# Two layers of cached attention and a gated feed-forward: the tail of one V load in each layer goes to loads of 8, 8 and 112 rows

## The chip, the cores and the metric

The kernel runs on one core of one Trainium2 chip, in one launch. The metric is the device time in microseconds; lower is better. Before the change it is 707.6 us, the median of three runs (707.39 to 707.8).

## The reference

A decoding step with one token for each of four sequences. Two layers, which share their weights and their cache, each compute attention over a cache of 4096 keys and a gated feed-forward, both on a normalised input and added to it:

```python
def _A_ref(x, k_cache, v_cache, wq, wo):        # x (4, 1, 512), caches (4, 8, 4096, 128)
    q = (x @ wq).reshape(B, Sq, 32, 128).transpose(0, 2, 1, 3)
    k = jnp.repeat(k_cache, 4, axis=1)
    v = jnp.repeat(v_cache, 4, axis=1)
    p = softmax(jnp.einsum("bhqd,bhkd->bhqk", q, k) * 128 ** -0.5)
    o = jnp.einsum("bhqk,bhkd->bhqd", p, v)
    return o.transpose(0, 2, 1, 3).reshape(B, Sq, 4096) @ wo

def _B_ref(x, w1, w3, w2):                      # 512 -> 1792 -> 512
    return (silu(x @ w1) * (x @ w3)) @ w2

for layer in range(2):
    x = x + _A_ref(layernorm(x), k_cache, v_cache, wq, wo)
    x = x + _B_ref(layernorm(x), w1, w3, w2)
```

Everything is float32.

## The kernel before, in words

One SBUF tile `arena` of 216 KB in each of 128 rows holds all that is loaded; `KB` is 256 floats, so one unit is 1 KB of a row. Loads stand in a list `plan`, written in the order in which they are to be issued, and `pump` (lines 136 to 150) issues from its front on the queue of SyncE as long as `take` finds room in the arena. `done` gives the room of a load back when its last piece has been used, and calls `pump` again. So the order of the transfers is the order of the list, and a transfer starts when TensorE has used up an earlier one. Each DMA bears on one of eight completion semaphores in turn.

The cache of one of the eight heads of K, or of V, is 8 MB: 64 KB in each of the 128 rows, as a rule one load (128 x 16384 floats). Layer 0 takes the heads 0 to 7, layer 1 takes them 7 to 0; the V of head 7 stays in the arena from one layer to the next, and so the V loads of layer 0 are of the heads 0 to 7, those of layer 1 of the heads 6 to 0. K of a head stands ahead of V of the head before it. Between the layers come the smaller loads of wo, w1, w3 and w2, at the end again w1, w3 and w2.

`scores` (line 342) multiplies the queries with K into `s_ps`; `factors` and `exponents` make the softmax of it, `turn_p` transposes the weights, and `weigh` (line 388) multiplies them with V into `o_ps`. `weigh` does it in two halves `f`, each of four pieces of V: the eight pieces, 8 KB of a row each, are the keys ("v", layer, head, 0 to 7). After the first half ScalarE empties `o_ps` (line 401), after the second VectorE does (line 403). TensorE goes through scores of one head, then V of the head before it, and waits for each load's completion semaphore before the first product that reads it.

In the names of the profile `arena<-in_v`, `arena<-in_kt`, `arena<-in_w` are these loads; line 143 issues them all, line 351 is a product with K and line 394 one with V.

Of the kernel before, what the change touches and what calls it, by code (L numbers as in the profile page):

```python
# [16 lines left out]
P = 128  # L17
# [12 lines left out]
KB = 256  # L30
ARENA = 216
TURN = HKV - 1
SPLIT = 3
SCRATCH = 64


@with_exitstack
def tile_decode_layers(ctx: ExitStack, tc: tile.TileContext, x, kt, v, wq, wo, w1, w3, w2, out):
    nc = tc.nc
# [5 lines left out]
    arena = const.tile([P, ARENA * KB], F32, name="arena")  # L45
# [9 lines left out]
    def take(n, at=None):  # L55
        if at is not None and at < WO:
            return at
        for i, (lo, size) in enumerate(free):
            if at is None and state["next"] > ring["to"]:

                end = min(lo + size, PT)
                if lo < WO + 4 and end > WO:
                    if WO - lo >= n:
                        end = WO
                    else:
                        lo = WO + 4
                if end - lo < n:
                    continue
                a = lo
                lo, size = free[i]  # L70
            else:
                a = lo if at is None else at
            if lo <= a and a + n <= lo + size:
                free[i:i + 1] = [(p, s) for p, s in ((lo, a - lo), (a + n, lo + size - a - n)) if s]
                return a
        return None
# [59 lines left out]
    def pump():  # L136
        while state["next"] < len(plan):
            src, per, keys, at = plan[state["next"]]
            n = src.shape[-1] // KB
            a = take(n, at)  # L140
            if a is None:
                return
            nc.sync.dma_start(arena[:, a * KB:(a + n) * KB], src)  # L143
            i = state["next"]
            if i == 0:
                nc.sync.dma_start(xt[:8], x[:8])
            left[i] = (len(keys), a, n)
            for j, key in enumerate(keys):
                where[key] = (a + j * per, per, i)
            state["next"] += 1  # L150
# [5 lines left out]
    def done(*key):  # L156
        i = where[key][2]
        k, a, n = left[i]
        left[i] = (k - 1, a, n)
        if k == 1:  # L160
            give(a, n)
            pump()

    def vacate(*key):
        a, n, _ = where[key]
        give(a, n)
        pump()

    xt = const.tile([P, KC, B], F32, name="xt")
    nc.scalar.dma_start(xt[8:], x[8:])  # L170
    pump()

    ident = const.tile([P, P], F32, name="ident")
# [425 lines left out]
```

## Time and profile before

| | |
|---|---|
| median of three runs | 707.6 us |
| the profiled execution | 708.3 us, of it a span of 706.5 us |
| TensorE's matmuls busy | 414.7 us (59%) |
| VectorE busy | 80.4 us (11%) |
| ScalarE busy | 38.3 us (5%) |
| moved by DMA | 299.37 MB, 424 GB/s in the mean |
| TensorE's granted clock, mean | 0.787 |

The span runs from the first to the last instruction; the profiled execution's own time is that and 1.8 us around it, and it is 0.7 us above the median. A row of a DMA queue gives its packets, its MB and the time of its packets as a share of 16 DMA engines over the span. A group's row gives busy time, the mean of one instruction in ns, and the idle time ahead of it with what ended most of that.

### The profile page before, as it was taken

To read this page: it belongs to the slowest core of one execution; us is meant where nothing else is said; L and a number is where in the kernel's file an instruction comes from. 1 tells how busy PE (TensorE), PEld (TensorE's weight loads), DVE (VectorE), ACT (ScalarE), POOL (GpSimd) and SP (SyncE) were. 2 spreads that over 40 slices of the span, in tenths; PEclk is the share of its full clock that TensorE was granted. 3 is DMA by queue.
4 is the path that set the end of the run, shared out by engine and by line. 5 is a ranking of instruction groups with operands and counts; after the bars stand their busy time and mean duration, and the time that the engine had idled before them with its cause. 6 is when DMAs were issued, how large, how long until landed. Compare 5 with 4: busy or idle time off the path is not lost. (4 is left out here: it accounts for less than half of the span.)

```text
span 706.5 us, 7210 instructions
## 1 busy us (share of the span) xinstructions
PE 414.7 (59%) x3250; PEld 147.4 (21%) x3250; DVE 80.4 (11%) x274; ACT 38.3 (5%) x87; POOL 2.9 (0%) x10
## 2 busy tenths in 40 slices
PE   3545354546555463547788886365564646367687
PEld 1111021112111120212243222021120212122235
DVE  2001010101001010101111021002010101010111
ACT  0000000000000000002010000000000000000101
POOL 0000000000000000000000000000000000000000
PEclk9977776777677687768899978679787878788679
DMA  9999999999999999999999999999999999999996
GB/s 384 459 405 468 416 423 450 423 428 438 439 423 428 453 416 438 446 401 435 407 404 371 407 437 448 430 428 435 434 424 449 424 423 454 427 416 428 423 425 283
DMA packets 13716, 299.37 MB, mean 424 GB/s; under 512 B 1655, under 2 KB 1783, under 8 KB 6007
## 3 DMA queue, kind: packets, MB, share of 16 engines
q1 hardware_dynamic: 13552, 298.92, 99.0%
q8 instruction: 25, 0.41, 0.2%
q10 hardware_dynamic: 135, 0.01, 0.0%
q14 instruction: 4, 0.03, 0.0%
HBM read 298.85 MB, written 0.07 MB: 423 GB/s over the span
## 5 line engine op out<-in xcount | busy, mean ns | idle before, releaser
L394 PE MATMUL o_ps<-arena 128*32 128x512 f32 x1024 | 149.4, 734 | 146.7 <-DMA arena<-in_v 132.2
L351 PE MATMUL s_ps<-arena,qpad 128*32 128x512 f32 x1024 | 151.5, 747 | 80.8 <-DMA arena<-in_kt 80.8
L394 PEld LDWEIGHTS o_ps<-arena 128*32 128x32 f32 x1024 | 37.8, 132 | 256.9 <-issue 226.1
L351 PEld LDWEIGHTS s_ps<-arena,qpad 128*32 128x32 f32 x1024 | 39.7, 133 | 174.7 <-issue 161.6
L403 DVE SCALAR_TENSOR_TENSOR p<-o_ps,parts,p 128x512 f32<-128x512 f32 x16 | 12.0, 751 | 270.6 <-PE o_ps L394 250.8
L358 DVE TENSOR_REDUCE top<-s_ps 128x1 f32<-128x512 f32 x16 | 11.1, 691 | 192.1 <-PE s_ps L351 192.1
L406 PE MATMUL m_ps<-sel,p 128*128 128x16 f32 x128 | 17.0, 265 | 14.3 <-DVE p L403 14.2
L415 PE MATMUL x_ps<-arena,oT 128*4 128x256 f32 x256 | 18.8, 431 | 6.3 <-DMA arena<-in_wo 4.3
L295 PE MATMUL o_ps<-arena,xpad 128*32 128x512 f32 x112 | 14.8, 649 | 12.0 <-DMA arena<-in_wq 12.0
L401 ACT ACTIVATE p<-o_ps,parts 128x512 f32<-128x512 f32 x16 | 11.0, 687 | 196.6 <-PE o_ps L394 187.9
L406 PEld LDWEIGHTS m_ps<-sel,p 128*128 128x128 f32 x128 | 15.5, 191 | 28.9 <-DVE p L403 28.9
L382 PE MATMUL t_ps<-ident,p 128*128 128x128 f32 x64 | 11.4, 305 | 13.5 <-ACT p L376 13.5
L369 ACT ACTIVATE f<-d 128x1 f32<-128x1 f32 x16 | 3.2, 203 | 252.8 <-DVE d L367 252.8
L376 ACT ACTIVATE p<-s_ps,top 128x512 f32<-128x512 f32 x16 | 10.9, 684 | 82.5 <-PE m_ps L406 82.5
L239 PE MATMUL m_ps<-ident,rows 128*32 128x128 f32 x70 | 13.1, 293 | 0.0
L383 DVE COPY arena<-t_ps 128x512 f32<-128x512 f32 x16 | 11.1, 691 | 8.8 <-PE t_ps L382 8.8
L382 PEld LDWEIGHTS t_ps<-ident,p 128*128 128x128 f32 x64 | 7.3, 150 | 19.5 <-ACT p L376 15.6
L446 PE MATMUL s_ps<-arena,xpad 128*32 128x192 f32 (+1 forms) x128 | 9.7, 421 | 1.4 <-DMA arena<-in_w 1.1
L446 PE MATMUL o_ps<-arena,xpad 128*32 128x192 f32 (+1 forms) x128 | 9.4, 404 | 1.3 <-DMA arena<-in_w 1.2
L239 PEld LDWEIGHTS m_ps<-ident,rows 128*32 128x32 f32 x70 | 8.3, 121 | 5.4 <-issue 3.0
L415 PEld LDWEIGHTS x_ps<-arena,oT 128*4 128x4 f32 x256 | 6.1, 93 | 15.3 <-DMA arena<-in_wo 5.0
L295 PEld LDWEIGHTS o_ps<-arena,xpad 128*32 128x32 f32 x112 | 3.5, 119 | 20.8 <-DMA arena<-in_wq 12.9
(94 smaller groups left out, 134.1 us busy)
## 6 DMA issues: line engine op xcount, KB each, us to landing
arena<-in_kt SPq DMA_DIRECT2D x4, 4096.0 KB, 18.5
arena<-in_v SPq DMA_DIRECT2D x4, 4096.0 KB, 39.0
arena<-in_kt SPq DMA_DIRECT2D x9, 1024.0 KB, 12.1
arena<-in_w SPq DMA_DIRECT2D x15, 512.0 KB, 8.6
arena<-in_wq SPq DMA_DIRECT2D x1, 7168.0 KB, 40.2
arena<-in_v SPq DMA_DIRECT2D x3, 2048.0 KB, 37.6
arena<-in_wo SPq DMA_DIRECT2D x1, 4096.0 KB, 24.2
arena<-in_kt SPq DMA_DIRECT2D x2, 2048.0 KB, 20.8
```

Source lines behind the costliest of these rows:

```text
L239: nc.tensor.matmul(m_ps[turn["m"] ^ 1][0:32, 384:512], rows, ident, start=True, stop=True)
L295: nc.tensor.matmul(ps[32 * k:32 * k + 32, :], xpad[:, k, lo:lo + 32], w[:, k, :], start=first, stop=last)
L351: nc.tensor.matmul(s_ps[32 * b:32 * b + 32, :], qpad[:, b, lo:lo + 32], k[:, j, :], start=(blk == 0), stop=(blk == NB - 1))
L358: nc.vector.tensor_reduce(top[:, 0:1], s_ps, axis=AX.X, op=ALU.max, negate=True)
L382: nc.tensor.transpose(t_ps[:, i, :], p[:, i * P:(i + 1) * P], ident)
L383: nc.vector.tensor_copy(pT.rearrange("p i r -> p (i r)"), t_ps.rearrange("p i r -> p (i r)"))
L394: nc.tensor.matmul(o_ps[32 * b:32 * b + 32, :], pT[:, i, 32 * b:32 * b + 32], w[:, b, :], start=(i == 0), stop=(i == NI - 1))
L401: nc.scalar.activation(p, o_ps, AF.Copy, scale=st["parts"][:, 0:1])
L403: nc.vector.scalar_tensor_tensor(p, o_ps, st["parts"][:, 1:2], p, op0=ALU.mult, op1=ALU.add)
L406: nc.tensor.matmul(flat(m), p[:, j * P:(j + 1) * P], sel[:, j].rearrange("p h b -> p (h b)"), start=(j == 0), stop=(j == 3))
L415: nc.tensor.matmul(x_ps[r:r + B, e * 256:e * 256 + 256], left(2 * i + n), w(n)[:, e * 256:e * 256 + 256], start=first, stop=last)
L446: nc.tensor.matmul(ps[32 * j:32 * j + 32, lo:lo + n], x32[:, k, :], w[:, j * n:(j + 1) * n], start=(k == 0), stop=(k == KC - 1))
```

## The change

A load whose first key stands in `SHARES` is split: its rows are loaded up to `m` KB as before, by one DMA of 128 rows, and the last 24 or 32 KB of each row by three more, of rows 0 to 7, 8 to 15 and 16 to 127. That is V of head 5 in layer 0 (64 = 40 + 24 KB of a row) and V of head 3 in layer 1 (32 + 32 KB). Bytes, places in the arena and everything computed are the same.

```diff
+SHARES = {("v", 0, 5, 0): 24, ("v", 1, 3, 0): 32}
...
-            nc.sync.dma_start(arena[:, a * KB:(a + n) * KB], src)
             i = state["next"]
+            m = n - SHARES.get(keys[0], 0)
+            nc.sync.dma_start(arena[:, a * KB:(a + m) * KB], src[:, 0:m * KB])
+
+            for lo, hi in ((0, 8), (8, 16), (16, P)) if m < n else ():
+                nc.sync.dma_start(arena[lo:hi, (a + m) * KB:(a + n) * KB], src[lo:hi, m * KB:])
             if i == 0:
                 nc.sync.dma_start(xt[:8], x[:8])
```

Lines below move down by five (394 becomes 399). On the queue of SyncE, around V of head 5 in layer 0 (the row 128x16384 of `in_v` that waits for DMAHW7; DMAHW0 to 7 are the completion semaphores, PE that of TensorE), there stood:

```order
L143 DMA arena<-in_v 128x16384 [waits DMAHW5_49,PE_49]
L143 DMA arena<-in_kt 128x16384 [waits DMAHW6_49,PE_49]
L143 DMA arena<-in_v 128x16384 [waits DMAHW7_49,PE_49]
L143 DMA arena<-in_kt 128x16384 [waits DMAHW0_49,PE_49]
L143 DMA arena<-in_v 128x16384 [waits DMAHW1_49,PE_49]
L143 DMA arena<-in_v 128x8192 [waits DMAHW2_49,PE_49]
```

Now there stands:

```order
L146 DMA arena<-in_v 128x16384 [waits DMAHW5_49,PE_49]
L146 DMA arena<-in_kt 128x16384 [waits DMAHW6_49,PE_49]
L146 DMA arena<-in_v 128x10240 [waits DMAHW7_49,PE_49]
L149 DMA arena<-in_v 8x6144 [waits PE_49]
L149 DMA arena<-in_v 8x6144
L149 DMA arena<-in_v 112x6144
L146 DMA arena<-in_kt 128x16384 [waits DMAHW0_49,PE_49]
L146 DMA arena<-in_v 128x16384 [waits DMAHW3_49,DMAHW2_49,DMAHW4_49,DMAHW1_49,PE_49]
```

One DMA has become four, and the V load two rows further on, which takes the room of this one, waits for four landings in place of one.

On TensorE, the products with V of head 5 in layer 0 (the rows with `o_ps`, ahead of them the scores of head 6) stood so:

```order
L351 MATMUL s_ps<-arena,qpad 32x512 [waits DMAHW0_49,DVE_49]
L351 MATMUL s_ps<-arena,qpad 32x512 x31
L394 MATMUL o_ps<-arena 32x512 [waits DMAHW1_49,DVE_49]
L394 MATMUL o_ps<-arena 32x512 x15
L394 MATMUL o_ps<-arena 32x512 [waits Activation_49]
L394 MATMUL o_ps<-arena 32x512 x15
L406 MATMUL m_ps_120<-sel,p 128x16 [waits DVE_49]
```

Now they stand so:

```order
L356 MATMUL s_ps<-arena,qpad 32x512 [waits DMAHW0_49,DVE_49]
L356 MATMUL s_ps<-arena,qpad 32x512 x31
L399 MATMUL o_ps<-arena 32x512 [waits DMAHW1_49,DVE_49]
L399 MATMUL o_ps<-arena 32x512 x15
L399 MATMUL o_ps<-arena 32x512 [waits Activation_49]
L399 MATMUL o_ps<-arena 32x512 x3
L399 MATMUL o_ps<-arena 32x512 [waits DMAHW4_49,DMAHW3_49,DMAHW2_49]
L399 MATMUL o_ps<-arena 32x512 x11
L411 MATMUL m_ps_120<-sel,p 128x16 [waits DVE_49]
```

The first 20 of the 32 products wait for the 128-row load alone, the last 12 for the three new loads as well. In layer 1 the same wait stands at the start of the second half, after 16 products.

## The prediction

> **What bounds the kernel now.** I read the page's head and DMA rows first, then the groups that wait, the chain, and last the stretches of the windows view.
>
> ```profile
> span 706.5 us, 7210 instructions
> DMA  9999999999999999999999999999999999999996
> q1 hardware_dynamic: 13552, 298.92, 99.0%
> q8 instruction: 25, 0.41, 0.2%
> q10 hardware_dynamic: 135, 0.01, 0.0%
> ...
> L394 PE MATMUL o_ps<-arena 128*32 128x512 f32 x1024 | 149.4, 734 | 146.7 <-DMA arena<-in_v 132.2
> L351 PE MATMUL s_ps<-arena,qpad 128*32 128x512 f32 x1024 | 151.5, 747 | 80.8 <-DMA arena<-in_kt 80.8
> ```
>
> The queue row says it: q1, which carries every load, takes 99.0% of 16 engines' span, and TensorE's two big groups stand idle 132.2 us for V and 80.8 us for K. No engine of the core is the bound. The last landing sets the end, as the chain's last pieces say:
>
> ```profile
> 628.95 43.48 DMA arena<-in_v
> ...
> 672.49 29.53 DMA arena<-in_w
> 702.02 0.14 issue
> 702.15 1.65 PE x_ps L502 x48
> ```
>
> A load is complete when the slowest of its DMA engines is, so what counts is not their mean but the last of the 16. The windows view shows how far apart they are (its last two columns are the busy share of the 16 engines and GB/s):
>
> ```profile
> core 0: us, PE busy (x) PEld busy (x) DVE busy (x) ACT busy (x) POOL busy (x), PEclk, DMA share, GB/s
> 180.00:240.00 60.00, 31.92 (x218) 9.58 (x214) 5.63 (x18) 1.87 (x5) 0.00 (x0) 0.70 1.01 435
> 372.00:378.00 6.00, 3.72 (x44) 1.68 (x48) 0.42 (x1) 0.00 (x0) 0.00 (x0) 0.89 1.02 400
> 378.00:384.00 6.00, 5.39 (x57) 2.41 (x49) 0.59 (x3) 0.00 (x0) 0.00 (x0) 0.83 1.00 365
> 384.00:390.00 6.00, 5.91 (x50) 3.37 (x54) 1.48 (x11) 0.85 (x3) 0.55 (x1) 1.00 0.96 337
> ...
> 698.00:699.00 1.00, 1.00 (x29) 0.80 (x33) 0.18 (x1) 0.00 (x0) 0.00 (x0) 1.00 0.97 389
> 699.00:699.50 0.50, 0.50 (x22) 0.50 (x12) 0.00 (x0) 0.00 (x0) 0.00 (x0) 1.00 0.83 336
> 700.00:700.50 0.50, 0.50 (x28) 0.45 (x24) 0.00 (x0) 0.00 (x0) 0.00 (x0) 1.00 0.54 217
> 701.00:701.50 0.50, 0.50 (x6) 0.34 (x4) 0.00 (x0) 0.00 (x0) 0.00 (x0) 1.00 0.54 188
> 701.50:702.00 0.50, 0.12 (x2) 0.00 (x0) 0.00 (x0) 0.00 (x0) 0.00 (x0) 1.00 0.35 135
> 702.50:703.00 0.50, 0.50 (x28) 0.50 (x20) 0.00 (x0) 0.00 (x0) 0.00 (x0) 1.00 0.07 25
> 703.00:703.50 0.50, 0.50 (x24) 0.25 (x16) 0.00 (x0) 0.00 (x0) 0.00 (x0) 1.00 0.00 0
> ```
>
> In steady state the 16 engines move 435 GB/s, 27.2 each. At the end all work until about 698.5 (0.97). By 700 to 700.5 the share is 0.54, nine of 16, and it is still 0.54 a microsecond later; the last one stops shortly before 703. So about seven engines are done some 3 us before the slowest. All carry the same bytes; what differs is small work such as the 25 instruction fetches (0.41 MB, 16 KB and so 0.6 us each at 27.2 GB/s). No view names the engines.
>
> **The change part by part.** First, which engines get what. The counts of the DMA rows tell it, with these:
>
> ```profile
> L143 SPq DMA_DIRECT2D arena<-in_kt x33: 327/328/607, 1.6 to 606.7; - x33
> L143 SPq DMA_DIRECT2D arena<-in_w x32: 327/328/837, 330.2 to 682.3; - x32
> L143 SPq DMA_DIRECT2D arena<-in_v x21: 327/328/425, 30.8 to 639.7; - x21
> L143 SPq DMA_DIRECT2D arena<-in_wo x5: 327/328/1021, 320.6 to 325.5; - x5
> L143 SPq DMA_DIRECT2D arena<-in_wq x2: 377/443/509, 0.7 to 2.4; - x2
> ```
>
> These are 93 loads of 128 rows, and with the store of the output 94 transfers. At one packet a row and one closing packet for each of 16 engines they make 94 x 144 = 13536 packets. q1 has 13552; the 16 left over are the one 8-row load of x: eight rows and eight closing packets, so eight engines with a row each. q10 agrees: 135 = 120 rows + 15. By the same division (the largest number up to 16 that divides the rows) the 112 rows go to 16 engines, seven each. Both new 8-row loads go, I take it, to the same eight engines. So of the tail, where each of 16 engines moved eight rows, eight engines ("the loaded eight") now move 1 + 1 + 7 = 9, and the others 7. At 27.2 GB/s a tail row of 24 KB (24,576 bytes) takes 0.90 us and one of 32 KB 1.20 us. The shift alone is thus 0.90 us more for the loaded eight and as much less for the others in layer 0, and 1.20 us each way in layer 1.
>
> Six more issues of 0.33 us lie on SP. They cost nothing, since SP then waits for TensorE, and the data engines are fed well ahead:
>
> ```profile
> 248.85 0.33 SPq L143 DMA_DIRECT2D arena<-in_v  x1
> 265.99 0.33 SPq L143 DMA_DIRECT2D arena<-in_kt  x1
> 276.56 5.85 PE L394 MATMUL o_ps<-arena 128*32 128x512 f32 x32 [10.63 <-DMA arena<-in_v]
> 286.98 0.33 SPq L143 DMA_DIRECT2D arena<-in_v  x1
> ...
> 579.28 6.38 PE L394 MATMUL o_ps<-arena 128*32 128x512 f32 x32 [10.10 <-DMA arena<-in_v]
> 586.52 3.64 PE L394 MATMUL o_ps<-arena 128*32 128x512 f32 x32 [0.86 <-ACT p L401]
> 590.23 0.33 SPq L143 DMA_DIRECT2D arena<-in_v  x1
> 599.04 1.94 PE L351 MATMUL s_ps<-arena,qpad 128*32 128x512 f32 x8 [4.84 <-DMA arena<-in_kt]
> ```
>
> SP issues nothing between 248.85 and 265.99; without that 17 us of cover the three would cost 1 us. The V load issued at 248.85 is in use at 276.56, 28 us later, when about one more load is queued.
>
> The wait that the change adds on TensorE, for the three tail loads, is behind work that can now start earlier: the first 40 or 32 of 64 KB land before the tail, so 10.63 us of idling becomes work begun earlier. That gains nothing by itself: the next product waits for its own load (4.84 us at 599.04). Were the tail late by more than that slack, the V product would delay the scores, but those wait for loads that are late by the same amount, since each DMA engine works its queue in order. Lateness of a DMA engine is therefore not hidden; it goes on to the end of the layer.
>
> Now the unknown cost. In a 128-row load 435 GB/s go to 128 rows: 27.2 GB/s to each engine, and as well 27.2 to each eight rows of SBUF. The rows do not tell to which of the two the limit belongs. If to the engine, an 8-row load takes 0.90 us (24 KB) or 1.20 (32 KB). If to eight neighbouring rows as a group, it takes eight times that: 7.2 or 9.6 us. These are the two ends. Nothing in this trace writes eight neighbouring rows from eight engines at length (the x load has 64 bytes a row), so no row is nearer to either; I take the mean, 4.05 and 5.4 us. The loaded eight are then later by 2 x 4.05 - 0.9 = 7.2 us in layer 0 and 2 x 5.4 - 1.2 = 9.6 us in layer 1. A gain from a faster 8-row load is excluded: no engine goes above 27.2 GB/s.
>
> The Trainium skill bears on this (SBUF — State Buffer, section "Door 1: The DMA port swizzle"): DMA bandwidth depends on how many of 16 ports the partitions reach; four neighbours, and the four 32 further on, share one, and partitions 0 to 3 alone got 27.6 GB/s. By it eight rows reach two ports and an 8-row load takes 3.6 or 4.8 us; by the same steps as below the time would be 717.8 us. No row here shows it.
>
> What comes off: at the end, seven engines have 3 us in hand, but eight are loaded, so at least one starts from the slower group, which ends 701.3 to 703: I take 2 us off in each layer at most, say 1.5 off layer 0 and 1.5 off layer 1. In the middle, between the layers, 400 GB/s falls to 365 and 337: (35 + 63) / 400 x 6 us = 1.5 us per engine, in which engines wait for issues and part of a delay can vanish. So 7.2 + 9.6 - 1.5 - 1.5 - 1.5 = +12.3 us. The profiled execution took 708.3 us, its span 706.5; the median of the runs is 707.6, and I add to that: 719.9, say **720 us**.
>
> **Rivals.** *No slowing of the 8-row loads, and no side wins.* The limit is the engine's. Then the loaded eight gain 0.90 and 1.20 us of work. Eight loaded against seven early means that one late engine at least gets more; if it is among the last, layer 1 ends 1.2 us later, if not up to 1.2 earlier. In layer 0 the like with 0.9. With opposite signs the time is 707.6 +- 1.4. For it: the last stretch holds one engine (0.07), of either kind. The same result comes if the change doesn't do what it says, because the 8-row loads use other engines each time: bytes then even out, 707.6.
>
> *Faster.* The limit is the engine's, and the loaded eight are the seven early ones and one of middling lateness. The others end 0.9 and 1.2 us sooner, and the early ones stay ahead (700.25 + 1.2 = 701.45, below 703 - 1.2 = 701.8). Time: 707.6 - 2.1 = 705.5. It decides as long as an 8-row load takes less than about twice 1.2 us: then the loaded eight are at 700.25 + 3.6 = 703.85, past today's end. For it: two groups, seven and nine, close to half and half. Against: nothing shows that the loaded eight are the early ones.
>
> *Slower by the shift alone.* The slowest engine is a loaded one in both layers: +2.1, 709.7.
>
> **How the numbers follow.** 0.2% of 707.6 is 1.4 us, about what can be told from no change. Slowed 8-row loads: 0.48, all slower. The limit the engine's: 0.52, of it 0.26 same, 0.21 faster, 0.05 slower by the shift alone. I put the two halves so near because the rows leave the limit open. So faster 0.21, same 0.26, slower 0.53; the likeliest single case gives 720. Its own range is wide: if an 8-row load takes twice its engine time (1.8 and 2.4), 2.7 + 3.6 - 4.5 = +1.8, about 709.4; at the upper end 13.5 + 18 - 4.5 = +27, 734.6; eight times in ten 711 to 729. With the other cases the range is 705.3 to 728: it leaves out what lies over 728 (0.08) and little below 705.3 (0.04).
>
> **What would show it.** After the change the V loads at 248.85 and 550.4 would show in the DMA share: around their landing (some 268 to 285, and 571 to 590) GB/s falls from 435 to below 330 for some microseconds when 8-row loads are slow, and stays near 435 when not. The V product after the tail would wait longer on in_v. In the last 10 us the drain gets longer than 4.5 us with about eight engines busy at its end; if I am wrong on the limit, the drain shrinks to about 3 us or just changes its order. The forecast falls if 8-row loads go at 27.2 GB/s an engine; it is too low if the 112-row load, seven rows an engine, is slowed as well.

## The result, and the profile after

The changed kernel takes 734.0 us (median of six runs, 733.63 to 734.44) against 707.9 us for the kernel before (median of six, 707.39 to 708.9): a ratio of 1.037, 95% interval 1.036 to 1.0381, or 26.1 us more. The forecast was 720 us, with a range up to 728: the measured time lies above it. The direction and the place (DMA, at the two split loads) came out; the rise is 26.1 us where 12.3 were forecast.

The page of the changed kernel, its span, the row of GB/s in 40 slices of 18.3 us, the queue of the loads and TensorE's two big groups:

```profile
span 732.6 us, 7221 instructions
GB/s 396 420 445 454 405 445 422 441 451 415 441 422 434 423 320 322 444 419 425 409 403 403 427 433 442 444 427 437 429 430 418 286 274 427 437 411 436 423 422 185
q1 hardware_dynamic: 13872, 298.92, 98.6%
L399 PE MATMUL o_ps<-arena 128*32 128x512 f32 x1024 | 153.7, 751 | 161.9 <-DMA arena<-in_v 147.9
L356 PE MATMUL s_ps<-arena,qpad 128*32 128x512 f32 x1024 | 150.8, 743 | 87.7 <-DMA arena<-in_kt 87.7
```

Two dips stand in the GB/s row, 320 and 322 at the split load of layer 0, 286 and 274 at that of layer 1; the last slice is the drain. The packets of the loads are busy for 98.6% of the span as before (99.0), although the span is 26 us longer and the bytes are the same 298.92 MB: the packets last longer, the engines do not stand idle. TensorE idles 15.7 us more for V and 6.9 us more for K, and its products are as many as before (1024 and 1024). The 320 packets more (13552 to 13872) are, for each layer, 8 + 8 and 8 + 8 for the two small loads and 112 + 16 for the third, 160 in all (rows, and one closing packet for each engine): that is what eight engines for 8 rows and sixteen for 112 give.

The windows view of the changed kernel (start and end, length, busy us of PE, PEld, DVE, ACT, POOL, TensorE's granted clock, busy share of the 16 DMA engines, GB/s); a packet is counted whole in the window in which it starts, so a share in a short window can pass 1:

```profile
265.00:270.00 5.00, 0.20 (x4) 0.00 (x0) 1.74 (x6) 0.20 (x1) 0.00 (x0) 1.00 0.97 179
270.00:275.00 5.00, 3.49 (x20) 1.01 (x24) 0.00 (x0) 0.00 (x0) 0.00 (x0) 0.52 0.97 226
275.00:280.00 5.00, 3.94 (x28) 0.72 (x20) 0.00 (x0) 0.69 (x1) 0.00 (x0) 0.80 1.10 257
280.00:285.00 5.00, 0.00 (x0) 0.00 (x0) 0.00 (x0) 0.00 (x0) 0.00 (x0) 0.89 1.02 256
285.00:290.00 5.00, 3.53 (x20) 1.05 (x24) 0.00 (x0) 0.00 (x0) 0.00 (x0) 0.50 0.97 419
...
264.00:304.00 40.00, 15.90 (x90) 5.21 (x82) 3.89 (x12) 1.67 (x4) 0.00 (x0) 0.71 1.02 336
560.00:610.00 50.00, 23.91 (x158) 7.53 (x158) 3.36 (x12) 1.67 (x4) 0.00 (x0) 0.69 1.00 313
...
720.00:724.00 4.00, 2.77 (x61) 1.78 (x65) 0.68 (x3) 0.00 (x0) 0.00 (x0) 1.00 0.49 195
724.00:726.00 2.00, 1.74 (x50) 1.46 (x46) 0.00 (x0) 0.00 (x0) 0.00 (x0) 1.00 0.17 59
726.00:728.50 2.50, 1.59 (x46) 1.35 (x38) 0.00 (x0) 0.00 (x0) 0.00 (x0) 1.00 0.06 25
```

The same view of the kernel before:

```profile
264.00:304.00 40.00, 21.36 (x150) 6.91 (x146) 3.89 (x12) 1.67 (x4) 0.00 (x0) 0.74 0.98 425
560.00:610.00 50.00, 30.51 (x222) 9.32 (x222) 5.63 (x18) 1.87 (x5) 0.00 (x0) 0.82 1.01 435
698.00:703.00 5.00, 4.46 (x113) 3.90 (x117) 0.18 (x1) 0.00 (x0) 0.00 (x0) 1.00 0.57 225
```

From 265 to 285 all 16 engines are busy (0.97 to 1.10) and move 179 to 257 GB/s, about half of what they moved with the same share before. In these windows this adds up to about the whole loss, with 435 GB/s as the full rate. In 40 us around layer 0's split the rate is 336 in place of 425: 40 x 89 / 435 = 8.2 us of work not done. In 50 us around layer 1's it is 313 in place of 435: 50 x 122 / 435 = 14.0 us. And the drain is longer: before, 0.43 of 5 us stood empty (2.15 us in the mean of the engines); now 0.51 of 4, 0.83 of 2 and 0.94 of 2.5 us, 6.05 together, 3.9 more. 8.2 + 14.0 + 3.9 = 26.1 us, and the spans differ by 732.6 - 706.5 = 26.1. That it fits to the tenth is luck: with 435 in place of 425 as the rate before at layer 0's place, the sum is 27.0.

The trace keeps the size and the duration of every packet, and a row of a tail is one packet. The 128 packets of 24 KB at layer 0's tail took 1.71 us in the median; with the tail as one load of 128 rows (the first experiment) they take 0.91. The first rows of the K load behind the tail, 64 KB each, took up to 5.5 us in place of 2.42.

On TensorE the wait has moved as the diff says (timeline, PE):

```profile
271.51 6.36 PE L399 MATMUL o_ps<-arena 128*32 128x512 f32 x32 [6.31 <-DMA arena<-in_v]
278.73 1.07 PE L399 MATMUL o_ps<-arena 128*32 128x512 f32 x8 [0.86 <-ACT p L406]
286.47 4.86 PE L399 MATMUL o_ps<-arena 128*32 128x512 f32 x24 [6.67 <-DMA arena<-in_v]
...
582.02 6.42 PE L399 MATMUL o_ps<-arena 128*32 128x512 f32 x32 [3.84 <-DMA arena<-in_v]
605.21 5.06 PE L399 MATMUL o_ps<-arena 128*32 128x512 f32 x32 [16.78 <-DMA arena<-in_v]
```

In layer 0 the product starts 5.1 us earlier than before (271.51 against 276.56, with the first 40 KB), and then stops for the tail until 286.47, when before all of this V had been there since 276.56. In layer 1 the tail comes at 605.21, when before the whole V was there at 579.28. (The timeline counts two for each product of the order: 32 + 8 = 40 are its 20, and 24 its 12.)

### The profile page after: what moved, and what is told of

Same layout as the page of the kernel before. It is cut to its first block, busy times and chain, and to the rows that moved or that the text cites. A ratio compares the mean times of both kernels' runs of the same rounds, so it can differ in the third digit from the quotient of the medians.

```text
span 732.6 us, 7221 instructions
## 1 busy us (share of the span) xinstructions
PE 415.3 (57%) x3250; PEld 147.0 (20%) x3250; DVE 80.3 (11%) x274; ACT 38.3 (5%) x87; POOL 2.9 (0%) x10
## 3 DMA queue, kind: packets, MB, share of 16 engines
q1 hardware_dynamic: 13872, 298.92, 98.6%
## 4 chain that ended last, share of the span: by engine, by line
DMA 74%; PE 21%; another core or an unknown queue 3%; ACT 1%; issue 1%; DVE 0%; SPq 0%; ACTq 0%
DMA arena<-in_v 54%; PE o_ps L399 15%; DMA arena<-in_w 7%; DMA arena<-in_wq 5%; DMA arena<-in_wo 4%; DMA arena<-in_kt 3%; PE s_ps L356 2%; PE o_ps L300 2%; ACT p L406 1%; PE m_ps L311 0%; PE m_ps L282 0%; PE x_ps L420 0%; SPq L146 0%; PE x_ps L507 0%
## 5 line engine op out<-in xcount | busy, mean ns | idle before, releaser
L399 PE MATMUL o_ps<-arena 128*32 128x512 f32 x1024 | 153.7, 751 | 161.9 <-DMA arena<-in_v 147.9
L387 PEld LDWEIGHTS t_ps<-ident,p 128*128 128x128 f32 x64 | 7.3, 151 | 18.3 <-ACT p L381 15.3
```

Of the source, the lines that this page charges most:

```text
L387: nc.tensor.transpose(t_ps[:, i, :], p[:, i * P:(i + 1) * P], ident)
L399: nc.tensor.matmul(o_ps[32 * b:32 * b + 32, :], pT[:, i, 32 * b:32 * b + 32], w[:, b, :], start=(i == 0), stop=(i == NI - 1))
```

## The experiments

All are the changed kernel with other pieces for the tail, or with one layer's split alone. The times are medians. The kernel before, run beside each of them, took 707.6 to 707.9 us.

### What it isn't: the split, or the addresses read

The tail as one load of 128 rows, in both layers:

```diff
-for lo, hi in ((0, 8), (8, 16), (16, P)) if m < n else ():
+for r in (slice(0, 128),) if m < n else ():
```

> The two tails (24 KB a row of V of head 5 in layer 0, 32 KB of V of head 3 in layer 1) are each one load of 128 rows. It keeps the split and the later wait on TensorE, and takes away the 8- and 112-row loads. Theory A (what costs is how the rows of a load fall on the receiving side): as before, 707.9 us, within 0.2%. Theory B (what costs is which rows are read at once from HBM): as before as well. Theory C (the split itself, more loads and a second wait, costs): most of the 26 us stays, 720 us or more.

Measured: 708.26 us, ratio 1.0003 (0.9994 to 1.0013). Its GB/s row has no dip:

```profile
GB/s 386 460 401 471 413 423 457 423 420 445 431 427 427 449 424 435 438 408 429 411 402 397 404 433 447 434 435 435 427 442 430 414 451 431 423 418 435 423 427 256
```

Theory C, under which the split itself costs, is out: the second load, its issue on SP, the second wait on TensorE and its restart cost nothing that can be measured. And the products that start earlier bring nothing. It is the division by rows.

The same 8, 8 and 112 rows, but with each tail in a tensor of its own, so that its rows lie one behind the other in HBM:

```diff
-nc.sync.dma_start(arena[lo:hi, (a + m) * KB:(a + n) * KB], src[lo:hi, m * KB:])
+nc.sync.dma_start(arena[lo:hi, (a + m) * KB:(a + n) * KB], tails[keys[0]][lo:hi])
```

> The changed kernel, but the two tails are read from tensors of their own, in which a row is 24 or 32 KB long and the next follows at once (before: 64 KB from row to row). The receiving side is the same. Theory A: 734 us as the changed kernel, within 1.5 us. Theory B: the slow part vanishes or changes by far more, 707 to 725 us. Theory C: 734 us.

Measured: 734.73 us, ratio 1.0371 (1.0353 to 1.039), the time of the changed kernel. For this kernel the source's layout is not the cause.

### Is it the 8-row loads at all?

112 rows and 16 rows, without a load of 8 (`slice(0, 112), slice(112, 128)`), and 64 and 64, where all 16 engines get the same bytes (`slice(0, 64), slice(64, 128)`):

> Both layers' tails are a load of 112 rows (seven an engine) and one of 16 (one an engine); there is no 8-row load and the engines carry equal bytes. In the changed kernel the 112-row load's rows took 1.7 us in place of 0.90 and 2.3 in place of 1.2. If that is its own price, 7 x 0.8 + 7 x 1.1 = 5.6 + 7.7 us, and the 16-row load adds 0.9 to 2.7 and 1.2 to 3.6: 722 to 728. If the 112-row load was only slow because the 8-row loads ran beside it or had set the engines apart: 708 to 714. Theory E: 708.

> Both layers' tails are two loads of 64 rows (0 to 63, 64 to 127); each runs on 16 engines, four rows each, so the engines carry equal bytes. Theory A: 64 rows reach half the groups, two engines share the room of one, each load at half speed: +7.2 in layer 0 and +9.6 in layer 1, 725. Theory A2: no loss, 708. Theory D: in each load half the engines write rows not theirs, 4 x 0.90 + 4 x 1.8 us in place of 8 x 0.90: +3.6 and +4.8, 716. Theory E: 708, all 16 engines have work.

Measured: 733.07 us (1.0354, 1.0309 to 1.0399) and 730.75 us (1.0321, 1.0291 to 1.0351). Windows of 112 and 16 rows:

```profile
268.00:274.00 6.00, 3.48 (x20) 1.03 (x24) 0.00 (x0) 0.00 (x0) 0.00 (x0) 0.72 0.91 225
...
264.00:304.00 40.00, 15.08 (x94) 4.83 (x82) 3.90 (x12) 1.67 (x4) 0.00 (x0) 0.71 1.02 333
560.00:610.00 50.00, 23.55 (x158) 7.42 (x158) 4.44 (x13) 1.67 (x4) 0.00 (x0) 0.73 1.01 319
```

and of 64 and 64:

```profile
268.00:274.00 6.00, 3.49 (x24) 1.05 (x28) 0.00 (x0) 0.00 (x0) 0.00 (x0) 0.72 0.96 205
...
264.00:304.00 40.00, 14.54 (x90) 4.67 (x82) 3.90 (x12) 1.67 (x4) 0.00 (x0) 0.70 1.01 340
560.00:610.00 50.00, 25.09 (x186) 8.88 (x187) 4.44 (x15) 2.44 (x6) 0.00 (x0) 0.76 1.01 320
```

Both times are above what was expected for a 112-row load with a price of its own (722 to 728) and for 64 rows at half speed (725). This settles the main thing that the prediction had wrong. A load of 112 rows without 8-row loads beside it, on all 16 engines, runs at 225 GB/s; the packets of this tail took 1.74 us in the median, against 0.91. By the sum used above, 112 and 16 rows lose 40 x (425 - 333) / 435 = 8.5 us and 50 x (435 - 319) / 435 = 13.3 us, 21.8 together; the changed kernel lost 22.2. With 8-row loads or without, the loss is nearly the same. And with the same bytes on every engine, 64 and 64 rows still lose 7.8 + 13.2 = 21.0 us: it is not an imbalance between the engines either. In both, each engine, though busy, goes at about half speed.

Two ways of dividing the first 32 rows into four loads of 8, neighbours or rows four apart, with 96 rows as the rest:

```diff
+for r in (slice(0, 8), slice(8, 16), slice(16, 24), slice(24, 32), slice(32, 128),) ...
```

```diff
+for r in (slice(0, 32, 4), slice(1, 32, 4), slice(2, 32, 4), slice(3, 32, 4), slice(32, 128),) ...
```

> The tails are four loads of 8 neighbouring rows (0 to 31) and one of 96 rows. Theory A (eight neighbours written at once share what two engines have): each 8-row load takes about 3.6 us (24 KB) and 4.8 us (32 KB) as in the changed kernel, so four take 14.4 and 19.2 us; 14.4 + 19.2 - 2 x 1.8 - 2 x 2.4 of the rows' own time (two rows more than the eight of before are carried by these engines) and what the 96-row load loses: 25 to 45 us above before, and about 25 us above its twin with rows four apart. Theory B (reading neighbours collides): like A for this one. Theory C: like the changed kernel, about 734 us, since the number of loads is about the same.

> As its twin with neighbouring rows, but each 8-row load takes every fourth row (0, 4, .. 28; then 1, 5, .. 29, and so on). Same bytes, same number of loads, same eight engines. Theory A: the eight rows lie apart on the receiving side, an 8-row load takes 0.90 and 1.2 us, four take 3.6 and 4.8; what is left is two rows more for eight engines (1.8 and 2.4 us) and the loss in the 96-row load: some 25 us below its twin. Theory B: only if reading at 256 KB apart is better than at 64 KB apart is it faster than the twin. Theory C: the same as its twin.

Measured: 741.4 us (1.0466, 1.045 to 1.0482) for neighbours and 734.74 us (1.0367, 1.0348 to 1.0386) for rows four apart. Neither came back to the time before, and they lie 6.7 us apart, not the 25 that theory A gave. Their windows at the tail of layer 0, neighbours first:

```profile
268.00:274.00 6.00, 3.75 (x20) 1.27 (x24) 0.00 (x0) 0.00 (x0) 0.00 (x0) 0.72 1.02 201
```

```profile
268.00:274.00 6.00, 3.72 (x21) 1.17 (x25) 0.00 (x0) 0.00 (x0) 0.00 (x0) 0.74 1.01 225
```

Here eight engines work on the small loads while the other eight already work on the 96 rows, and both kernels are slow. What the small loads lose and what the 96 rows lose can't be told apart in these. The next four have no large piece.

### Which rows get in each other's way

In layer 0 alone the tail goes as 16 loads of 8 rows, in four patterns. They come one behind the other on eight engines (a share of 0.5):

```diff
 # far16: rows four apart
+for r in (slice(0, 32, 4), slice(1, 32, 4), slice(2, 32, 4), slice(3, 32, 4), slice(32, 64, 4), ...
 # near16: neighbours
+for r in (slice(0, 8), slice(8, 16), slice(16, 24), ...
 # step2: rows two apart
+for r in (slice(0, 16, 2), slice(1, 16, 2), slice(16, 32, 2), slice(17, 32, 2), ...
 # step16: rows sixteen apart
+for r in (slice(0, 128, 16), slice(1, 128, 16), slice(2, 128, 16), ...
```

Rows four apart:

> Only layer 0's tail (24 KB a row of V of head 5) is split: into 16 loads of 8 rows four apart (0, 4, .. 28; 1, 5, .. 29; .. 99, .. 127), so that eight DMA engines carry all of it and the other eight none. In a 128-row load the engines that now carry all write rows 0 to 63, if rows fall to the engines in fours. Theory A (each group of rows takes in one engine's rate, and no more): no two of the eight meet, so 0.90 us a row throughout, 14.4 us of work in place of 7.2: +7 us, 715. Theory D (an engine is slow, for itself, when it writes rows that another engine writes in a 128-row load): the loads of rows 0 to 63 at 0.90 us a row, those of 64 to 127 at about 1.8: 21.6 us, +14, 722. Theory E (whenever a load does not run on all 16 engines the rest runs at half speed): 1.8 us throughout, 28.8 us, +21, 729.

Neighbours:

> As its twin, but the 16 loads are of 8 neighbouring rows (0 to 7, 8 to 15, .. 120 to 127); layer 0 alone, eight engines carry all. Theory A, four engines on the room of one: 3.6 us a row, 57.6 us in place of 7.2: +50, 758. Theory A2 (a group of rows takes in two engines' rate, which the 1.85 us of the 8-row loads beside the 96-row load speak for): 1.8 us a row, 28.8 us, +21, 729. Theory D: most rows are another engine's: 1.8 us, 729. Theory E: 729, and the same as its twin.

Two apart:

> Layer 0 alone: the tail of 24 KB a row as 16 loads of 8 rows, two apart (rows 0, 2, ... 14; then 1, 3, ... 15; and so on). Loads of 8 neighbours gave 1.65 us a row and 735.4 us, loads of 8 rows four apart 0.92 us a row and 720.5. Here two engines are in each group of four neighbours at a time. Theory A (one engine's rate for each group of four rows): 1.8 us a row while nothing else runs, about 735 us. Theory B (the limit is of pairs or smaller, as 1.65 in place of 3.6 us for neighbours may mean): 0.92 us a row at first, slower only where the next K load runs beside it, 720 us.

Sixteen apart:

> Layer 0 alone: the tail of 24 KB a row as 16 loads of 8 rows, sixteen apart (rows j, j + 16, ... j + 112), so that each load has both p and p + 32 in it, and p + 64 and p + 96. Theory A (rows p and p + 32 take one engine's rate together): two engines meet in each of four pairs, 1.8 us a row while nothing else runs, about 735 us. Theory B (only neighbours share): 0.92 us a row, about 720 us.

Measured: 720.51 us four apart (1.0176, 1.0145 to 1.0208), 735.35 neighbours (1.0386, 1.0308 to 1.0464), 727.26 two apart (1.0276, 1.0256 to 1.0297), 730.95 sixteen apart (1.0328, 1.0308 to 1.0349). Both of the first two lie between their theories (715, 722 and 729; 729 and 758). The windows of rows four apart, while only the eight engines work and then with the next K load beside them:

```profile
268.00:276.00 8.00, 6.16 (x40) 1.49 (x40) 0.14 (x1) 0.69 (x1) 0.00 (x0) 0.79 0.49 209
280.00:286.00 6.00, 0.00 (x0) 0.00 (x0) 0.00 (x0) 0.00 (x0) 0.00 (x0) 0.50 0.95 210
```

of neighbours:

```profile
268.00:274.00 6.00, 3.75 (x24) 1.18 (x28) 0.00 (x0) 0.00 (x0) 0.00 (x0) 0.72 0.50 107
274.00:280.00 6.00, 2.42 (x24) 0.30 (x15) 0.00 (x0) 0.69 (x1) 0.00 (x0) 1.00 0.46 107
```

of rows two apart:

```profile
268.00:274.00 6.00, 4.12 (x20) 1.13 (x24) 0.23 (x2) 0.20 (x1) 0.00 (x0) 0.58 0.45 143
274.00:280.00 6.00, 3.52 (x24) 0.61 (x16) 0.00 (x0) 0.69 (x1) 0.00 (x0) 0.85 0.53 180
```

and of rows sixteen apart:

```profile
268.00:274.00 6.00, 3.91 (x24) 1.20 (x28) 0.63 (x3) 0.20 (x1) 0.00 (x0) 0.72 0.43 98
274.00:280.00 6.00, 2.19 (x20) 0.29 (x12) 0.00 (x0) 0.69 (x1) 0.00 (x0) 0.98 0.51 123
```

In these windows, and in far16 until 276, eight engines work on the tail and next to nothing runs beside them (until 269.4 a few last rows of the piece ahead). What they reach differs with the rows:

| rows of one load | who would meet, with all eight engines at the same load | GB/s of eight engines, 268 to 274, then 274 to 280 |
|---|---|---|
| four apart, 0, 4, ... 28 | one engine in each of eight groups of four neighbours | 209 (268 to 276) |
| two apart, 0, 2, ... 14 | two in each of four groups | 143, 180 |
| neighbours, 0 to 7 | four in each of two groups | 107, 107 |
| sixteen apart, 0, 16, ... 112 | rows p and p + 32 in four pairs | 98, 123 |

The eight are not all at the same load, as the packets show: in near16 five engines begin the first small load at 265.9 to 266.3 us and three at 267.6 to 268.4, when the five are at their second. Sixteen apart, that changes little, since four loads on end use the same groups of rows. There the commonest duration of a packet is 1.85 us, twice the 0.92 of far16. So, where they meet, two engines that write rows p and p + 32 get together what one gets alone (2 x 24,576 bytes in 1.85 us are 26.6 GB/s, one packet in 0.92 us is 26.7). That was theory A of the pattern sixteen apart; its time is 731 and not 735, and some of its packets took less, down to 0.92. For neighbours and rows two apart, how many engines meet at a time is not shown, so these rows give no price for a group of four; two apart, the rate rises from 143 to 180 under the same pattern, and the time, 727 us, fits neither theory.

One rival stands untested here: the rows of a load lie apart in HBM too, 64 KB for neighbours and 1 MB for rows sixteen apart. The run with the tails in tensors of their own varied that for 8, 8 and 112 rows alone.

The second window of far16 is the more telling one for the changed kernel. Once the next K load runs on the other eight engines, the share goes to 0.95 and the rate stays at 210: sixteen engines move what eight moved. The tail's packets then take about 1.9 us in place of 0.92, and the first rows of K 4.5 to 4.9 in place of 2.42. The tail is then in rows 64 to 127; the first of these still went at the full rate while nothing ran beside them, so theory D, by which they are slow for themselves, is out. That the other eight engines write those same rows of K would fit it, but no view names the rows of an engine.

Two statements of the Trainium skill can be held against this. The Trainium skill (SBUF — State Buffer, section "Door 1: The DMA port swizzle") says that a row and the one 32 further on share a port, and that rows 0 to 63 get no more than rows 0 to 31, about 218 GB/s. The trace agrees: 26.6 GB/s for such a pair, and 205 GB/s for the load of 64 rows. It also gives 27.6 GB/s to rows 0 to 3 alone; no run here shows that, since the eight engines are not at the same rows at once. The Trainium skill (DMA: Bandwidth & Descriptors, section "The descriptor swizzle") says that in a transfer of 128 rows each engine writes one such port, and none meets another. That would be why the 128-row tail costs nothing and every other division tried does; the runs show the speeds, not the assignment.

### Do the layers add up?

```diff
-SHARES = {("v", 0, 5, 0): 24, ("v", 1, 3, 0): 32}
+SHARES = {("v", 0, 5, 0): 24}        # layer0
+SHARES = {("v", 1, 3, 0): 32}        # layer1
```

> The 8, 8 and 112 rows in layer 0 alone (tail of 24 KB a row), layer 1 as before. The changed kernel's landings were 9.9 us late right behind layer 0's tail and 8.0 to 8.4 us late at the V loads two heads on and later. Theory (each layer's delay stays in the transfers until the end, none is lost between the layers): 707.9 + 8.0 to 9.9 = 716 to 718 us. Rival (the prediction's take-offs: the pauses between the layers and the engines in hand swallow some 3 to 4 us of it): 711.5 to 714. On record from the prediction's own terms: +7.2 - 1.5 = 713.6, or less.

> The 8, 8 and 112 rows in layer 1 alone (tail of 32 KB a row), layer 0 as before. In the changed kernel the lateness grew there from 8.3 to 25.9 us of landing. Theory (the delays of the two layers add up): +17.6, 725.5 us, and with layer 0 alone the two sum to about +26. Rival (something in the changed kernel hides part, or one layer's delay feeds the other): the two alone sum to clearly more or less than 26, by more than 3 us. The prediction's own terms would give +9.6 - 1.5 = 716.0.

Measured: layer 0 alone 718.16 us (1.0149, 1.0133 to 1.0165), so +10.55; layer 1 alone 722.15 us (1.0213, 1.0193 to 1.0234), so +14.5. Together 25.1, with intervals of 9.4 to 11.7 and 13.6 to 16.6, against 26.1 for both. The windows of layer 0 alone, then of layer 1 alone:

```profile
264.00:304.00 40.00, 14.98 (x94) 4.95 (x86) 3.89 (x12) 1.67 (x4) 0.00 (x0) 0.71 1.02 337
```

```profile
560.00:610.00 50.00, 23.11 (x158) 7.24 (x150) 3.89 (x12) 1.67 (x4) 0.00 (x0) 0.74 1.01 329
```

Layer 0's loss at its own place is 40 x (425 - 337) / 435 = 8.1 us, and 10.55 us arrive at the end: nothing of it is seen to vanish between the layers, and the rival (711.5 to 714 us) is out. The expectation for layer 1, +17.6 from how late the last landing was, was 3 us too high; the loss there, 50 x (435 - 329) / 435 = 12.2 us, is a mean over the engines, and the end is set by the last one.

No version beat the kernel before. Among those that move the tail by rows, the 8, 8 and 112 rows in layer 0 alone are the cheapest, and moving it as 128 rows is the same as not splitting.

## Why the prediction was wrong, point by point

- **DMA is the bound and its lateness is not hidden: right.** Layer 0 alone loses 8.1 us at its place and 10.55 at the end.
- **Which engines: right.** 320 packets more, and a share of 0.43 to 0.53 wherever only 8-row loads run.
- **The split itself at nothing: right.** 128 rows as a second load: 1.0003.
- **The 112-row load at "27.2 GB/s an engine": this is the step that failed.** From the count "16 engines, seven each" the prediction went on to "a tail row of 24 KB takes 0.90 us". It had the rate from 128-row loads only. 112 rows run at 225 GB/s (with the 16 left over as one load), so 112 x 24,576 bytes take 12.2 us and not 6.3; the packets say the same, 7 x 1.74 = 12.2. That alone is 5.9 us in layer 0 and, for rows of 32 KB at the same rate, 16.3 in place of 8.4 us, 7.9 more in layer 1: 13.8 us which the sum has nowhere. The prediction named it as what would make it too low, and gave it neither a rival nor a term.
- **The 8-row loads: slow, but over-sized.** It asked whether the limit belongs to the engine or to eight neighbouring rows as a group (0.90 to 7.2 us), and took the mean, 4.05. Eight neighbours moved 107 GB/s with nothing beside them: 8 x 24,576 / 107,000 = 1.84 us; what they took beside the 112 rows was not read by itself. The 3.6 us that the prediction gives for eight rows on two ports is twice that. With 1.84 the term of layer 0 is 2 x 1.84 - 0.9 = 2.8 in place of 7.2; with 32 KB in proportion, 2 x 2.45 - 1.2 = 3.7 in place of 9.6. So 16.8 us of the sum should have been 6.5. Without this error the forecast would have been 10.3 us lower still, at 709.6: the two errors partly cancelled. And that the range's upper end for 8-row loads at 7.2 us, 734.6, lies next to the measured 734.0 is chance: they took a quarter of that.
- **The 4.5 us taken off: wrong.** The engines' 3 us in hand and the slack in the middle took off nothing that shows. The prediction read 365 and 337 GB/s in the middle as engines that wait, but the shares in its own lines there are 1.00 and 0.96: they were busy. And each layer alone costs at the end more than its mean loss (10.55 against 8.1, 14.5 against 12.2), and the drain lost 3.9 us more in place of giving 3.
- **The sum with the measured terms:** 13.8 + 6.5 = 20.3 us, taking off nothing, against 26.1 measured. The 5.8 us left are not broken down; the sum has no term for what runs beside the tail, and the K load behind it is slowed too (its first rows took up to 5.5 us in place of 2.42).
- **The rivals.** "No slowing of the 8-row loads", "faster" and "by the shift alone" all rested on engines that keep their rate whatever the rows, and fell with that: 64 and 64 rows give each engine the same bytes and still cost 22.9 us.
- **What would show it: as said,** GB/s below 330 at both places and a drain longer than 4.5 us with about eight engines (0.49) in it; at the very end one was left (0.06).

## What to carry to other kernels

A DMA rate read from loads of 128 rows holds for loads of 128 rows. A load of any other division must be priced from a row of its own kind, or else, as a first guess, by half the rate, as 112, 96 and 64 rows went here. Look at busy share and GB/s side by side: a full share at half the GB/s says that packets last longer, and where the engines hinder each other, as here, shifting rows between engines does not help. To split a load, split it by columns and keep all 128 rows: that was free here.

## What the runs showed of the hardware that was not expected

- Loads of 112, 96 and 64 rows, all on 16 busy engines, moved 225, 201 to 225 (beside loads of 8) and 205 GB/s, against 435 with 128 rows.
- Two engines on rows p and p + 32 share one engine's rate: a row of 24 KB takes 1.85 us where they meet, in place of 0.92. The HBM side of that pattern was not varied.
- A load with such rows slows what runs beside it, and is slowed by it: in far16 the rate stayed at 210 GB/s when eight more engines joined, and a 64 KB row of the K load took 4.5 to 4.9 us in place of 2.42.
